# A table of ones 64 or 256 bytes wide: where the buffers behind it begin, in decay attention with two feed-forward layers

## The chip, the cores and the metric

The kernel runs on one core of one Trainium2 chip. The metric is the time of one execution on the device, in microseconds (us); lower is better. TensorE is called PE here, VectorE DVE, ScalarE ACT, GpSimd POOL and SyncE SP, as in the profile.

## The reference, cut to what matters

```python
# q, k, v: (2, 8, 768, 64) float32; lam: 8 decays; 768 tokens in blocks of 64
for b in range(nb):
    qb, kb, vb = (q[:, :, sl], k[:, :, sl], v[:, :, sl])
    intra = np.einsum('bhij,bhjd->bhid', np.einsum('bhic,bhjc->bhij', qb, kb) * Dmask[None], vb)
    inter = np.einsum('bhid,bhde->bhie', qb * lam_pow[None], kv_state)
    out[:, :, sl] = intra + inter
    kv_state = lam_block * kv_state + np.einsum('bhsd,bhse->bhde', kb * rev_pow[None], vb)
# x: the 1536 tokens by 512 channels of out
xn = x / np.sqrt(np.mean(x * x, -1, keepdims=True) + 1e-06) * rms_g
g = xn @ w_gate
x = (g * sigmoid(g) * (xn @ w_val)) @ w_out          # 512 -> 1536 -> 512
out = np.maximum(np.maximum(x @ w1, x @ w2), x @ w3) @ w_out2   # 512 -> 768 -> 512
```

All weights of the two feed-forward layers come as 64-bit floats, rms_g and the input of the attention as 32-bit ones.

## The kernel before, in words

The 1536 tokens are cut into 12 chunks of 128. For each chunk the attention is worked out in steps: `turn` transposes keys and queries on PE, `scores` multiplies them, `masked` and `next_state` run on DVE, `mixed` makes the output of the chunk, `summed` and `normed` scale it, and `rest` leaves it as a pair of a high and a low part (`xh`, `xl`), since every product of the feed-forward layers is made of three matmuls on such pairs. The first seven chunks go through a fixed interleaving ahead of the feed-forward work (the last loop of the program); the other five are slipped in between the matmuls of the first feed-forward stage (`first_stage`), which takes the first four column groups of w_gate and w_val. `second_stage` does the rest, on PE without a break.

Weights come as raw 64-bit words and are turned into a pair of 32-bit tiles in a unit of work of its own: ACT takes both halves of the words (L252, L253), DVE puts them together (L209 to L216), POOL adds (L219), ACT and POOL split the sum into a high and a low part (L180, L183). Every engine works its instructions off in the order written.

All loads are issued by SP, in one order. A chunk has three loads of 256 KB, one each for k, q and v (`load`, L92); each brings 8 runs of 256 bytes to each of 128 partitions, one run for each head. A raw weight tile of 4096 bytes a partition is brought by `load_to` (L170): for w_gate and w_val in three DMAs of runs of 1024 bytes, for the others in one DMA with runs of 1024 or 4096 bytes. The issues stand in this order at the start: k and q of chunk 0, then v, k and q of the next ones up to q of chunk 3, the first raw tile of w_gate, v of chunk 3 and so on. SP takes a load only when the buffer it goes to is free.

On-chip memory is given out by pools, one behind the other, in bytes of each partition. Pools `act` and `wp` come first; in `wp` lie three of the five buffers of raw weights. Then come `attc` (constants of the attention), `ld` (three buffers each for k and q, four for v, and two further buffers of raw weights) and `att` (working tiles of the attention). The last three are given back after the attention, and two new pools take their place from the same first byte. In `attc` each tile begins at a multiple of 32 bytes behind the last, in this order: lam8, lamh, g_sb, ones, ident, zeros, mhalf, Tm, lami, diag.

The table `ones` is set by one memset (L962) at the start, and read in one place alone, its first column as the moving operand of the matmul in `summed` (L403):

```python
nc.tensor.matmul(out=pm[:, 0:1], lhsT=d["ss"][:, a, :], rhs=ones[:, 0:1], start=a == 0, stop=a == n - 1)
```

`load_to` chooses the buffer of a raw tile by its number in the list of weights; `more` holds for numbers 3, 4, 8 and 9 alone:

```python
more = pos["load"] % 5 > 2 and pos["load"] < 3 * PLAIN - 2
t = (ld if more else wp).tile([P, KD, 2 * P], I32, tag="raw", name="wraw", bufs=2 if more else 3)
```

Of the kernel before, what the change touches and what calls it, by code (L numbers as in the profile page):

```python
# [9 lines left out]
F32 = mybir.dt.float32  # L10
# [8 lines left out]
P = 128  # L19
# [7 lines left out]
def tile_decay_attention_swiglu_maxout(  # L27
# [25 lines left out]
    C = P // 2  # L53
# [11 lines left out]
    attc = att_ctx.enter_context(tc.tile_pool(name="attc", bufs=1))  # L65
# [9 lines left out]
    lam8 = attc.tile([P, H], F32, name="lam8")  # L75
    lamh = attc.tile([P, NP], F32, name="lamh")
    g_sb = attc.tile([P, KD], F32, name="g_sb")
    ones = attc.tile([P, C // 4], F32, name="ones")
    ident = attc.tile([P, P], F32, name="ident")
    zeros = attc.tile([P, P], F32, name="zeros")  # L80
    mhalf = attc.tile([P, 1], F32, name="mhalf")
# [964 lines left out]
```

## Time and profile before

| | |
|---|---|
| median of 3 runs | 555.02 us (554.21 to 555.48) |
| the profiled execution | 553.67 us, of it 551.9 us from the first to the last instruction |
| PE busy | 534.0 us, 97% of the span |
| DVE, ACT, POOL busy | 371.4, 279.3 and 300.9 us |
| moved by DMA | 44.67 MB in 65598 packets |

The page has a strip of 40 slices of the span for each engine, for the clock that PE was granted (PEclk, in tenths of full speed) and for the DMA engines. PE is full in nearly every slice; the slices that are not full lie in the first 100 us, where chunks of the attention are worked on, and in the last. The DMA engines are busiest in the first fifth of the span and have long gaps after it.

### The profile page before, as it was taken

How to read it: one execution, taken by the hardware profiler on the slowest of the kernel's cores; microseconds unless marked ns; L12 is line 12 of the kernel's file. 1: busy time of each engine (PE TensorE's matmuls, PEld its weight loads, DVE VectorE, ACT ScalarE, POOL GpSimd, SP SyncE). 2: the span in 40 equal slices, each digit the busy share in tenths (PEclk: the TensorE clock that was granted, in tenths of full speed). 3: DMA queues.
4: the chain of work that ended last, by engine and by line, in shares of the span. 5: the costliest groups of instructions: out<-in, count | busy, mean ns of one | idle time of the engine just before them, and what ended most of it. 6: DMA issues, size and time to landing. Idle time of an engine off the chain costs nothing.

```text
span 551.9 us, 9738 instructions
## 1 busy us (share of the span) xinstructions
PE 534.0 (97%) x3728; PEld 440.6 (80%) x3728; DVE 371.4 (67%) x680; ACT 279.3 (51%) x541; POOL 300.9 (55%) x247
## 2 busy tenths in 40 slices
PE   7799997999999999999999999999999999999997
PEld 7687765878888888888888888888888888888886
DVE  4577775454886687677777685787677577684364
ACT  3576675245355556546347525646466755551120
POOL 2266886323434567475546726886386544962050
PEclk8898999999999999999999999999999999999999
DMA  9895926300111222231221312120222322210015
GB/s 183 209 225 168 220 75 133 60 3 0 39 38 40 76 76 77 77 113 41 77 76 39 114 40 76 40 76 8 69 77 83 110 76 70 84 38 1 0 40 190
DMA packets 65598, 44.67 MB, mean 81 GB/s; under 512 B 40080, under 2 KB 61840, under 8 KB 65552
## 3 DMA queue, kind: packets, MB, share of 16 engines
q1 hardware_dynamic: 64848, 44.05, 29.8%
q8 instruction: 29, 0.48, 0.4%
q14 instruction: 17, 0.14, 0.1%
q10 hardware_dynamic: 704, 0.01, 0.1%
HBM read 40.90 MB, written 3.15 MB: 80 GB/s over the span
## 4 chain that ended last, share of the span: by engine, by line
PE 84%; issue 4%; POOL 4%; DVE 2%; DMA 2%; ACT 1%; SPq 1%; POOLq 0%; ACTq 0%; DVEq 0%
PE p L683 34%; PE acc L874 9%; PE r L683 8%; PE acc L480 6%; PE acc L481 6%; PE acc L482 6%; PE pv L490 5%; PE q L683 4%; PE pg L490 4%; POOL W L219 2%; PE px L377 1%; SPq L170 1%; DMA qn<-in_q_dram 1%; POOL kd L287 1%; DMA wraw<-in_moe_w_gate_dram 1%
## 5 line engine op out<-in xcount | busy, mean ns | idle before, releaser
L183 POOL TENSOR_TENSOR wl<-W,wh 128x512 fp32r<-128x512 f32 x77 | 100.7, 1309 | 58.7 <-ACT wh L180 58.7
L219 POOL TENSOR_TENSOR W<-W,wraw 128x512 int32<-128x512 int32 x60 | 80.6, 1343 | 70.2 <-DVE W L216 66.0
L180 ACT CAST wh<-W 128x512 fp32r<-128x512 f32 x77 | 47.8, 621 | 82.3 <-POOL W L219 80.6
L501 POOL TENSOR_TENSOR hl<-sg,hh 128x512 fp32r<-128x512 f32 x36 | 47.2, 1310 | 36.1 <-ACT hh L500 36.1
L683 PE MATMUL p<-xh,wh 128*128 128x512 f32 x148 | 57.6, 389 | 0.0
L683 PE MATMUL p<-xl,wh 128*128 128x512 f32 x148 | 57.6, 389 | 0.0
L683 PE MATMUL p<-xh,wl 128*128 128x512 f32 x148 | 57.6, 389 | 0.0
L480 PE MATMUL acc<-hh,wh 128*128 128x512 f32 x144 | 56.7, 394 | 0.7 <-DVE W L216 0.7
L481 PE MATMUL acc<-hl,wh 128*128 128x512 f32 x144 | 56.2, 390 | 0.0
L482 PE MATMUL acc<-hh,wl 128*128 128x512 f32 x144 | 56.1, 390 | 0.0
L252 ACT ACTIVATE W<-wraw 128x512 f32<-128x512 f32 x60 | 40.3, 672 | 9.2 <-DMA wraw<-in_moe_w_gate_dram 5.1
L838 DVE TENSOR_TENSOR acc_sb<-acc,acc_sb 128x512 f32<-128x512 f32 x46 | 31.7, 690 | 19.5 <-PE acc L482 18.3
L209 DVE TENSOR_SCALAR mid<-W 128x512 f32<-128x512 f32 x58 | 39.7, 685 | 3.3 <-ACT W L252 3.3
L212 DVE TENSOR_SCALAR mid<-mid 128x512 int32<-128x512 int32 x58 | 40.2, 693 | 0.8
L216 DVE SCALAR_TENSOR_TENSOR W<-wraw,mid 128x512 int32<-128x512 int32 x58 | 39.5, 681 | 1.1
L253 ACT ACTIVATE wraw<-wraw 128x512 int32<-128x512 uint32 x60 | 39.8, 664 | 0.0
L738 ACT COPY c<-p 128x512 f32<-128x512 f32 x34 | 20.0, 587 | 38.3 <-PE p L683 38.3
L501 POOL TENSOR_TENSOR hl<-m,hh 128x512 fp32r<-128x512 f32 x18 | 24.1, 1345 | 23.0 <-ACT hh L500 22.9
L683 PE MATMUL p<-yh,wh 128*128 128x512 f32 x90 | 35.0, 389 | 0.0
L683 PE MATMUL p<-yl,wh 128*128 128x512 f32 x90 | 35.0, 389 | 0.0
L683 PE MATMUL p<-yh,wl 128*128 128x512 f32 x90 | 35.0, 389 | 0.0
L500 ACT CAST hh<-sg 128x512 fp32r<-128x512 f32 x36 | 22.3, 620 | 24.1 <-DVE sg L624 18.1
(176 smaller groups left out, 1327.7 us busy)
## 6 DMA issues: line engine op xcount, KB each, us to landing
wraw<-in_moe_w_out_dram SPq DMA_DIRECT2D x18, 512.0 KB, 3.4
wraw<-in_moe_w_dram SPq DMA_DIRECT2D x18, 512.0 KB, 3.5
kn<-in_k_dram SPq DMA_DIRECT2D x12, 256.0 KB, 5.3
qn<-in_q_dram SPq DMA_DIRECT2D x12, 256.0 KB, 5.5
vn<-in_v_dram SPq DMA_DIRECT2D x12, 256.0 KB, 5.3
wraw<-in_moe_w_gate_dram SPq DMA_DIRECT2D x12, 256.0 KB, 3.0
wraw<-in_moe_w_gate_dram SPq DMA_DIRECT2D x24, 128.0 KB, 3.1
wraw<-in_moe_w_val_dram SPq DMA_DIRECT2D x12, 256.0 KB, 3.1
```

The source lines that it names most:

```text
L180: nc.scalar.copy(out=wh, in_=W.bitcast(F32))
L183: nc.gpsimd.tensor_tensor(out=wl, in0=W.bitcast(F32), in1=wh.bitcast(F32), op=ALU.subtract)
L212: nc.vector.tensor_scalar(out=mid[key], in0=mid[key], scalar1=0x07FFFFFF, scalar2=3, op0=ALU.bitwise_and, op1=ALU.logical_shift_left)
L219: nc.gpsimd.tensor_tensor(out=W, in0=W, in1=lo, op=ALU.add)
L252: nc.scalar.activation(out=W.bitcast(F32), in_=hi.bitcast(F32), func=AF.Abs)
L480: nc.tensor.matmul(out=out, lhsT=wh, rhs=xh_, start=first, stop=False)
L481: nc.tensor.matmul(out=out, lhsT=wh, rhs=xl_, start=False, stop=False)
L482: nc.tensor.matmul(out=out, lhsT=wl, rhs=xh_, start=False, stop=last)
L490: nc.tensor.matmul(out=ps, lhsT=w[:, kk * P:(kk + 1) * P], rhs=x[:, kk, :], start=n == 0, stop=n == len(todo) - 1)
L501: nc.gpsimd.tensor_tensor(out=dst_l, in0=src, in1=dst_h.bitcast(F32), op=ALU.subtract)
L683: nc.tensor.matmul(out=ps, lhsT=w[:, ks], rhs=r[:, o + k, :], start=first and k == 0 and n == 0, stop=k == 1 and n == 2, skip_group_check= ...
L874: nc.tensor.matmul(out=acc[:, cs], lhsT=x[:, ts], rhs=w[:, cs], start=n == 0, stop=n == len(todo) - 1)
```

## The change

One constant gets another width. C is 64, so that `ones` has 64 columns (256 bytes a partition) where it had 16 (64 bytes).

```diff
-    ones = attc.tile([P, C // 4], F32, name="ones")
+    ones = attc.tile([P, C], F32, name="ones")
```

No instruction is added, taken away or moved on any engine; the memset of L962 writes 128x64 elements in place of 128x16. What changes is where the tiles behind `ones` begin: 192 bytes later, up to the end of the pool `att`. Taken modulo 256, the places in the two built programs are these:

| tiles | first byte mod 256 before | after |
|---|---|---|
| ident, zeros, mhalf | 32 | 224 |
| Tm, lami, diag | 64 | 0 |
| k, q, v (10 buffers of 2048 bytes) | 64 | 0 |
| raw weights in `ld` (2 buffers of 4096 bytes) | 64 | 0 |
| kT, qT, qs, kd, A, S, sq, x | 64 | 0 |
| raw weights in `wp` (3 buffers), and all else in `act` and `wp` | 128 | 128 |
| the pools that follow the attention | 128 | 128 |

A run of k, q or v is 256 bytes long, so that each one lay across a multiple of 256 before and lies between two of them after. Of 60 raw weight tiles, four (numbers 3, 4, 8 and 9 of the list) go to buffers that move.

## Rows read from the trace of the kernel before

**Rows 1.** The page: busy time by engine, and strips of 40 slices.

```profile
PE 534.0 (97%) x3728; PEld 440.6 (80%) x3728; DVE 371.4 (67%) x680; ACT 279.3 (51%) x541; POOL 300.9 (55%) x247
...
PEclk8898999999999999999999999999999999999999
DMA  9895926300111222231221312120222322210015
```

**Rows 2.** Stretches in us: busy time by engine, granted PE clock, DMA share, GB/s.

```profile
20.00:25.00 5.00, 2.84 (x18) 2.60 (x18) 2.66 (x8) 3.97 (x11) 0.00 (x0) 0.75 0.82 213
...
60.00:90.00 30.00, 26.52 (x354) 20.36 (x354) 24.68 (x58) 20.31 (x44) 23.80 (x22) 1.00 0.47 120
90.00:100.00 10.00, 7.57 (x41) 5.68 (x42) 2.66 (x8) 2.91 (x5) 6.55 (x7) 0.83 1.20 223
...
150.00:540.00 390.00, 390.00 (x1723) 322.92 (x1722) 271.90 (x436) 199.29 (x361) 223.09 (x172) 1.00 0.20 63
```

**Rows 3.** Who waited for whom, PE and ACT: us in total, times, longest.

```profile
PE pm L403 <- ACT x L390: 2.2, 1, 2.2
PE pk L297 <- DMA kn<-in_k_dram: 1.9, 1, 1.9
...
PE sc L321 <- ACT x L390: 1.5, 1, 1.5
...
PE pq L299 <- DMA qn<-in_q_dram: 0.6, 1, 0.6
...
ACT W L252 <- DMA wraw<-in_moe_w_gate_dram: 5.1, 1, 5.1
```

**Rows 4.** Timeline: start, us, engine, line, operation; idle before in brackets.

```profile
0.81 0.07 DVE L962 MEMSET ones<- 128x16 f32 x1 [0.81 <-PEq L1030]
0.86 0.17 DVE L963 MEMSET zeros<- 128x128 f32 x1
...
1.08 4.21 PE L968 MATMUL warm<-zeros 128*128 128x128 f32 x18 [1.08 <-DVE zeros L963]
...
5.94 0.42 PEld L299 LDWEIGHTS pq<-ident,qn 128*128 128x128 f32 x4 [0.32 <-DMA qn<-in_q_dram]
```

**Rows 5.** Timeline of SP's queue: the last loads ahead of the first raw tile.

```profile
10.38 1.24 SPq L92 DMA_DIRECT2D kn<-in_k_dram  x1
11.71 2.41 SPq L92 DMA_DIRECT2D qn<-in_q_dram  x1
14.17 2.37 SPq L170 DMA_DIRECT2D wraw<-in_moe_w_gate_dram  x3
```

**Rows 6.** DMA queues from 3.7 to 4.7 us: packets, MB, share of 16 engines.

```profile
q1 hardware_dynamic: 909, 0.23, 101.5%
q10 hardware_dynamic: 271, 0.00, 15.0%
```

**Rows 7.** DMA queue of SP from 73.8 to 74.3 us, a raw tile in `wp`.

```profile
q1 hardware_dynamic: 165, 0.16, 95.5%
```

**Rows 8.** DMA queue of SP from 54.8 to 55.3 us, raw tile 8, in `ld`.

```profile
q1 hardware_dynamic: 165, 0.16, 99.5%
```

**Rows 9.** DMA packets from 91.3 to 91.9 us, k of chunk 10 alone.

```profile
DMA packets 673, 0.17 MB, mean 285 GB/s; under 512 B 673, under 2 KB 673, under 8 KB 673
...
q1 hardware_dynamic: 673, 0.17, 125.6%
```

**Rows 10.** DMA packets from 5 to 14 us, k, q and v load after load.

```profile
DMA packets 7912, 1.97 MB, mean 219 GB/s; under 512 B 7911, under 2 KB 7911, under 8 KB 7911
...
q1 hardware_dynamic: 7751, 1.96, 133.5%
```

**Rows 11.** Copies of ACT by line: durations in ns, min/median/max.

```profile
L303 ACT COPY qT<-pq x12: 585/587/643, 6.6 to 110.5; 128x512 f32<-128x512 f32 x12
...
L738 ACT COPY c<-p x34: 576/587/612, 176.1 to 522.9; 128x512 f32<-128x512 f32 x34
```

**Rows 12.** Stretches round the two idle times of PE, columns as in rows 2.

```profile
23.90:27.30 3.40, 3.29 (x72) 3.09 (x75) 1.97 (x7) 2.51 (x5) 1.14 (x2) 0.50 1.01 237
27.30:30.70 3.40, 3.40 (x87) 3.28 (x82) 2.17 (x8) 1.82 (x7) 2.96 (x3) 0.70 1.14 249
...
94.30:97.70 3.40, 3.40 (x11) 2.87 (x12) 0.69 (x1) 1.16 (x3) 3.40 (x3) 0.52 1.37 222
```

## The prediction

> **What bounds the kernel now.** I read the page first, then the busy time by stretches, then the waits, then the DMA packets. The page shows PE busy for 97% of the span [rows 1]; the stretches show where the rest is: from 150 to 540 us PE is busy for the whole 390 us at full clock, with DMA at a fifth of its time [rows 2]. Nothing that the change does to a load can be felt there. PE loses time in the first 100 us, where the strip of the DMA engines is nearly full too [rows 1]. The list of waits names two places where a load of the kinds that move is the cause. Near 21 us ACT stands 5.1 us before the first raw tile of w_gate (L252); the scaling of a chunk (x, L390) is queued behind it on ACT, and PE stands 2.2 us for that [rows 3]. Near 92 us PE stands 1.9 us for k of chunk 10 and 0.6 us for its q [rows 3]. [...]
>
> **The memset.** The two memsets of DVE give a price: 0.07 us for 16 columns, 0.17 us for 128 [rows 4], so 0.10 / 112 us a column, and 48 more columns take 0.04 us. The memset of zeros and with it the 9 warming matmuls start 0.04 us later [rows 4]. The transposes follow these on PE, and the second set of them waits 0.32 us for the first q anyway [rows 4], which covers the 0.04 us; without that cover the price would be 0.04 us, under 0.01% of the time. I count nothing.
>
> **Tiles of the engines.** Does an engine work faster on a tile at a multiple of 256? ACT's copy of 128x512 takes 587 ns into qT, which lies at 64 modulo 256, and 587 ns into c, at 128 [rows 11]. Place makes no difference there, and I count nothing for kT, qs, kd, A, S, x and the constants either. Room is no matter: the pools behind the attention keep their place.
>
> **The loads: one packet.** This is the one term that can be of size. A packet is one run, and the share of the 16 engines' time gives its duration. From 3.7 to 4.7 us, 909 packets of 256 bytes took 1.015 x 16 x 1000 ns, 17.9 ns each; beside them 271 packets of 4 bytes (g_sb, on ACT's queue) took 0.150 x 16000 / 271 = 8.9 ns each [rows 6]. In a raw tile of `wp` 159 packets of 1024 bytes and 6 of 4 bytes took 0.955 x 16 x 500 ns, so 47.7 ns each [rows 7]. I count the bytes in steps of 32. From 4 to 256 bytes are 7 steps in 9.0 ns, 1.29 ns a step; from 256 to 1024 bytes are 24 steps in 29.8 ns, 1.24 ns a step. A 4-byte packet cannot lie across a multiple of 256 bytes, each run of k, q and v did. If lying across cost something, the first difference would stand out by it. At 1.24 ns a step the first 7 steps make 8.7 ns, and 0.3 ns is left for lying across. [...] The raw tiles say the same: a tile in `ld` at 64 modulo 256 takes (0.995 x 8000 - 4 x 9) / 161 = 49.2 ns a packet and one in `wp` at 128 takes 47.7 [rows 7, 8]. So the place within 256 bytes does not show; I take 0.3 ns as the saving, the row nearest to the case, with 0 and 1.0 as its near ends.
>
> [...]
>
> **The loads: a stretch.** A shorter packet helps only if packets set the pace. From 91.3 to 91.9 us, 673 packets passed 16 engines in 600 ns: one in 14.3 ns on each, less than the 17.9 ns that each takes, so they overlap [rows 9]. From 5 to 14 us 7751 packets passed in 9 us, one in 18.6 ns [rows 10]. The runs lie at the same place modulo 256 in both, so what slows the long row to 18.6 ns is not the place alone, and may well be something that the change leaves as it is. The difference, 4.3 ns, is the most that I grant the change for a packet in that row; the least is nothing.
>
> **What it comes to.** SP issues the loads of 5 to 14 us without a pause, each taking about 1.2 us or longer, and the first raw tile follows at 14.17 us [rows 5]. Ahead of it lie 7751 / 16 = 484 packets on each engine [rows 10]. At 0.3 ns they save 0.15 us of ACT's wait and so of PE's. At 92 us two loads of 64 packets on each engine save 2 x 64 x 0.3 ns = 0.04 us. The sum is 0.2 us, with 0 and 0.6 us (1.0 ns) as its ends. The profiled execution took 553.67 us, 551.9 of them its span, and would take 553.5 us; it lies 1.35 us under the median, which the change is compared with. So I take the 0.2 us from the median: 555.02 - 0.2 = 554.8 us. The runs before spread over 1.27 us, and a measurement of this kernel can tell about 0.2% (1.1 us) from no change. The forecast is no change that can be told, 553.9 to 556.1 us.
>
> **Rival 1: the packets do get shorter, and the time with them.** Mechanism: a run that lies across a multiple of 256 bytes makes two writes, and where load follows load the writes set the pace. Halfway between nothing and 4.3 ns, 2.2 ns a packet, saves 484 x 2.2 ns = 1.1 us of the 2.2 us that PE stands near 21 us, and 128 x 2.2 ns = 0.3 us near 92 us: 555.02 - 1.4 = 553.6 us. At 4.3 ns it is 2.1 + 0.55 us, and the clock may stay up. PE is busy for 6.7 us from 23.9 to 30.7 us at 0.50 and 0.70 [rows 12], (0.50 + 0.30) x 3.4 = 2.7 us of lost clock, of which I let half come back, since ACT and DVE have their own work there: 555.02 - 2.65 - 1.35 = 551.0 us. So 551.0 to 553.8 us. For it speaks that the DMA strip is full where the loads matter [rows 1]; against it the packets of 4, 256 and 1024 bytes, and that the dense row at 14.3 ns had the same place.
>
> [...]
>
> **Rival 2: slower, by one more stretch at the lower clock.** Near 84 us PE stands 1.5 us for x of ACT [rows 3], and the clock stays at 1.00 over 60 to 90 us [rows 2]; after the waits of 2.2 and 2.5 us it fell. ACT takes raw weights and x in a fixed order, so that a raw tile which lands later against the rest by 0.7 us or more would lengthen the 1.5 us to some 2.2 us, and I take that as the point from which the clock falls here too. Price: 0.7 us of idle time, and 3.4 us at half clock as in 94.3 to 97.7 us [rows 12], which loses 1.7 us: 555.02 + 2.4 = 557.4 us; if loads nearby only shift the half-clock stretch without more idle time, 556.7 us. For it speaks that every load moves a little against the compute; against it that the change makes no load longer by any row, and moves them by tenths at most.
>
> **Rival 3: it does not do what it says.** Of 60 raw tiles four move, and none of the 36 loads of k, q and v is left out; the one raw tile that ACT stands 5.1 us for is number 0, in `wp`, which keeps its place. It only comes earlier through the loads ahead of it. If place did matter for 1024 bytes alone, four tiles are all, none of them waited for in rows 3: 555.0 us. This lies within the forecast and has no share of its own.
>
> **How the numbers follow.** Forecast (0 to 0.6 us saved, and the scatter of three runs): 0.56. Rival 1: 0.29. Rival 2: 0.15. The predicted time is 554.8 us. The range reaches down to 552.4 us, which takes in rival 1 at its middle and leaves out its far end (about 0.10), and up to 556.4 us, which leaves out most of rival 2 (about 0.10). Rival 1 lies below 553.9 us nearly whole: faster 0.29; slower 0.15; same 0.56.
>
> **What would show it.** In the trace after, the share of the 16 engines and the count of packets of 3.7 to 4.7 us, of 5 to 14 us and of 91 to 92 us, worked out as here: 17.9, 18.6 and 14.3 ns again if I am right; 15 to 16 ns a packet, or a long row at 14 to 17 ns, if rival 1 is. The wait of ACT for the first raw tile should stay near 5.1 us, or fall by 1 us and more; PE's waits of 2.2, 1.9 and 0.6 us with it. The clock from 20 to 31 us and from 94 to 98 us shows what came back, and a further dip near 85 us would show rival 2. The prediction is wrong if the long row turns out to be set by the writes, or if the 0.2 us shift where a clock stretch begins.

## The result, and the profile after

The changed kernel takes 548.71 us (median of 4 runs, 547.21 to 549.46) beside 554.62 us of the kernel before on the same chip (552.30 to 555.48): a ratio of 0.9897, with an interval of 0.9858 to 0.9935. So it is faster, by 3.6 to 7.9 us, some 1%. A second comparison on another chip, with 12 runs of the changed kernel and 27 of the kernel before, gave 549.1 against 552.3 us, 0.9947 (0.9929 to 0.9965). By the medians the gain is 5.9 and 3.2 us; the second rests on more runs. The forecast was 554.8 us and no change; the range ended at 552.4 us.

The page of the kernel after, to be read beside [rows 1]: the span is 547.5 us where it was 551.9. PE has 2.8 us less of busy time, so some of its matmuls ran at a higher clock (the mean granted clock of the two profiled executions is 0.984 before and 0.991 after); the rest of the 4.4 us is idle time that has gone. In the strip of the DMA engines the first ten slices add up to 47 tenths where it was 51.

```profile
span 547.5 us, 9738 instructions
...
PE 531.2 (97%) x3728; PEld 438.5 (80%) x3728; DVE 371.3 (68%) x680; ACT 279.2 (51%) x541; POOL 301.0 (55%) x247
...
PEclk8899998999999999999999999999999999999999
DMA  8987717000201231141221212121123222200015
```

The DMA packets of the kernel after from 5 to 14 us, the stretch of [rows 10]: number, bytes, share of 16 engines.

```profile
DMA packets 8688, 2.16 MB, mean 241 GB/s; under 512 B 8687, under 2 KB 8687, under 8 KB 8687
...
q1 hardware_dynamic: 8515, 2.15, 105.8%
```

In 9 us 8515 packets passed SP's queue where 7751 did before. One passed each engine every 9000 x 16 / 8515 = 16.9 ns instead of 18.6, and took 1.058 x 16 x 9000 / 8515 = 17.9 ns instead of 24.8. From 5 to 11 us, where there are loads of k, q and v alone, the pair is 16.0 and 17.8 ns; the kernel before (the second row) has 18.5 and 24.8 ns there:

```profile
q1 hardware_dynamic: 5994, 1.51, 111.3%
```

```profile
q1 hardware_dynamic: 5195, 1.31, 134.3%
```

The two places that were to show no difference show none: from 3.7 to 4.7 us a packet takes 0.942 x 16000 / 844 = 17.9 ns, as in [rows 6], and k of chunk 10, which comes some 4 us earlier in this kernel (87.1 to 87.7 us), passes at one packet in 9600 / 676 = 14.2 ns, as in [rows 9] (first and second row):

```profile
q1 hardware_dynamic: 844, 0.21, 94.2%
...
q1 hardware_dynamic: 676, 0.17, 126.3%
```

Five more loads follow that one without a pause. The fifth load of the six, q of chunk 11, does show a difference. In the kernel before (95.5 to 96.6 us, the first row) one packet passes in 17600 / 967 = 18.2 ns and takes 25.2 ns; in the kernel after (91.3 to 91.9 us, the second row) it is 9600 / 660 = 14.5 ns and 17.9 ns:

```profile
q1 hardware_dynamic: 967, 0.24, 138.5%
```

```profile
q1 hardware_dynamic: 660, 0.17, 123.2%
```

SP issues the first raw tile at 12.54 us instead of 14.17 [rows 5], and ACT takes it up at 19.25 us. Timeline of ACT after, start, duration and, in brackets, the idle time ahead with what ended it:

```profile
19.25 0.68 ACT L252 ACTIVATE W<-wraw 128x512 f32<-128x512 f32 x1 [3.31 <-DMA wraw<-in_moe_w_gate_dram]
...
25.23 0.68 ACT L252 ACTIVATE W<-wraw 128x512 f32<-128x512 f32 x1 [1.67 <-DMA wraw<-in_moe_w_val_dram]
```

Before, the first of these stood at 21.03 us after a wait of 5.07 us:

```profile
21.03 0.67 ACT L252 ACTIVATE W<-wraw 128x512 f32<-128x512 f32 x1 [5.07 <-DMA wraw<-in_moe_w_gate_dram]
```

It is 1.78 us earlier, and PE's wait for x is 0.9 us where it was 2.2 [rows 3]. Of the waits of PE after, none names a DMA any more; near 90 us ACT has taken the place of k and q of chunk 10 (the third and fourth row, in place of 1.9 and 0.6 us):

```profile
PE sc L321 <- ACT x L390: 1.4, 1, 1.4
...
PE pm L403 <- ACT x L390: 0.9, 1, 0.9
...
PE pk L297 <- ACT wh L180: 1.3, 1, 1.3
...
PE pq L299 <- ACT kT L301: 0.8, 1, 0.8
```

Where the 4.4 us arise is seen when the same matmul is looked up in both traces. The matmul behind PE's wait for x is 1.7 us earlier in the kernel after (21.6 against 23.35 us), one at 29.2 us of before 2.8 us, one at 46.2 us 4.1 us, one at 93.1 us 4.6 us, one at 100 us 4.3 us, and the last 4.4 us. So next to nothing is gained after 50 us. The lead does not only grow: it is back to 2.2 us at 35.5 us, where PE of the kernel after waits 0.5 us for x, and 3.1 us at 43.6 us. The steps from 1.7 to 2.8 and from 3.1 to 4.1 us lie in two stretches of clock. Before, PE ran at 0.50 of its clock from 22.5 to 29.3 us, and again from 43.0 to 46.4 us; after, only from 22.5 to 25.9 us. (In both kernels a further stretch follows the idle time near 90 us.) Windows of the kernel after: us, busy time of PE, PEld, DVE, ACT and POOL, granted clock, DMA share, GB/s. The first pair answers to [rows 12]:

```profile
23.90:27.30 3.40, 3.40 (x104) 3.33 (x105) 3.24 (x12) 2.07 (x6) 2.73 (x3) 0.71 0.95 231
27.30:30.70 3.40, 3.29 (x124) 2.96 (x125) 2.62 (x8) 2.87 (x7) 1.40 (x2) 1.00 0.85 216
43.00:46.40 3.40, 3.13 (x73) 2.38 (x73) 3.40 (x7) 2.44 (x9) 1.51 (x2) 1.00 0.85 282
...
90.80:94.20 3.40, 3.40 (x9) 2.61 (x8) 0.69 (x1) 0.92 (x2) 2.44 (x2) 0.50 1.01 238
```

The third window (43.0 to 46.4 us) in the kernel before:

```profile
43.00:46.40 3.40, 3.29 (x58) 2.36 (x62) 3.05 (x8) 2.03 (x4) 3.19 (x4) 0.50 0.96 267
```

The time of one run goes with its mean granted clock. The 93 runs of the kernel before that stand beside the experiments have a median of 554.0 us where the mean clock is 0.983 to 0.985 (16 runs), 552.9 at 0.986 to 0.988 (21), 552.1 at 0.989 to 0.991 (40) and 550.8 at 0.992 to 0.994 (7): some 0.35 us for 0.001. The kernel after takes 549.5 us at 0.991 (median of 5 runs, 549.2 to 551.1) and 548.6 us at 0.993 to 0.994 (7 runs). So some 2.2 to 2.6 us of the gain are there at equal clock; the rest goes with a higher clock of the changed kernel (a mean of 0.992 over the 12 runs of the second comparison, 0.988 over the 93). This need not be a cause apart from the loads: one stretch of 3.4 us at half clock, as from 43.0 to 46.4 us, takes 0.5 x 3.4 / 552 = 0.003 off the mean of a run, and the traces have three to five such stretches in the four kernels with all loads at 64, 128 or 192 and no filling matmuls, and one to three with all loads at 0 (the last microseconds, after PE's work, left out).

### The profile page after: what moved, and what is told of

It is laid out like the page before. It is cut to its first block, busy times and chain, and to the rows that moved or that the text cites. A ratio compares the mean times of both kernels' runs of the same rounds, so it can differ in the third digit from the quotient of the medians.

```text
span 547.5 us, 9738 instructions
## 1 busy us (share of the span) xinstructions
PE 531.2 (97%) x3728; PEld 438.5 (80%) x3728; DVE 371.3 (68%) x680; ACT 279.2 (51%) x541; POOL 301.0 (55%) x247
## 4 chain that ended last, share of the span: by engine, by line
PE 86%; POOL 3%; issue 2%; DVE 2%; ACT 2%; DMA 2%; SPq 2%; POOLq 0%; ACTq 0%; DVEq 0%
PE p L683 34%; PE acc L874 9%; PE r L683 8%; PE acc L480 6%; PE acc L481 6%; PE acc L482 6%; PE pv L490 5%; PE pg L490 4%; PE q L683 4%; PE px L377 1%; SPq L92 1%; POOL W L219 1%; DMA wraw<-in_moe_w_gate_dram 1%; SPq L170 1%; PE pq L299 1%
## 5 line engine op out<-in xcount | busy, mean ns | idle before, releaser
L252 ACT ACTIVATE W<-wraw 128x512 f32<-128x512 f32 x60 | 40.3, 672 | 8.3 <-DMA wraw<-in_moe_w_gate_dram 3.8
L500 ACT CAST hh<-sg 128x512 fp32r<-128x512 f32 x36 | 22.3, 620 | 24.6 <-DVE sg L624 18.6
```

The costliest lines, as they stand in the source:

```text
L252: nc.scalar.activation(out=W.bitcast(F32), in_=hi.bitcast(F32), func=AF.Abs)
```

## Experiments

Three theories stood against each other. **A**: a run of a load that does not begin at a multiple of 256 bytes costs more on its way into the on-chip memory. **B**: the engines work faster on the tiles of `att` and `attc` that moved. **C**: PE's clock alone, for which a load that lands a little earlier is enough. Each run stands beside the kernel before on its own chip; "pace" is the time between two packets on one DMA engine from 5 to 11 us and "duration" what a packet takes there, both worked out as above.

### The loads alone, the tiles alone

`ones` keeps its 64 bytes. Empty tiles move the pool `ld` alone to 0 modulo 256 (the first), or the tiles of `att` alone (the second).

```diff
-    diag = attc.tile([P, C], F32, name="diag")
+    diag = attc.tile([P, C], F32, name="diag"); attc.tile([P, 48], F32, name="pad1"); att.tile([P, 16], F32, name="pad2", bufs=1)
```

> Only the pool of loads moves: k, q, v and two raw tiles begin at 0 modulo 256, ones stays 64 bytes wide, the constants and the working tiles of the attention stay at 64 modulo 256 (unused filler tiles of 192 and 64 bytes see to that). Theory A (runs of k, q, v that no longer lie across a multiple of 256 bytes pass faster where load follows load): the whole gain, ratio 0.990, and 16 ns or less between packets from 5 to 14 us, 18.0 ns a packet. Theory B (engines read or write the working tiles and constants faster at 0): ratio 1.000, 18.6 ns between packets and 24.8 ns a packet as before.

```diff
-    diag = attc.tile([P, C], F32, name="diag")
+    diag = attc.tile([P, C], F32, name="diag"); att.tile([P, 48], F32, name="pad2", bufs=1)
```

> Only the working tiles of the attention (kT, qT, qs, kd, A, S, sq, x) move to 0 modulo 256; k, q, v, raw tiles and constants stay at 64. Theory A: ratio 1.000 and 18.6 ns between packets from 5 to 14 us. Theory B: a ratio below 0.995 at unchanged packets.

With the loads alone: 547.48 against 552.37 us, 0.9918 (0.9897 to 0.9940); pace 15.6 ns, duration 17.8 ns. With the tiles alone: 551.72 us, 0.9992 (0.9974 to 1.0011); pace 18.4 ns, duration 24.3 ns. SP's queue from 5 to 11 us, the loads alone:

```profile
q1 hardware_dynamic: 6153, 1.55, 114.3%
```

and the tiles alone:

```profile
q1 hardware_dynamic: 5227, 1.32, 132.4%
```

The whole gain is in the loads: the first kernel leaves the constants and the tiles of `att` at their old places. Theory B falls. The loads alone were run once more beside later experiments:

> The kernel in which only the pool of loads moves to 0, once more, on the same chip as the three before: 0.990 to 0.995. It should be no slower than the changed kernel if constants and working tiles take no part.

549.82 us, 0.9936 (0.9906 to 0.9966), pace 16.7 ns. The two results agree within their intervals.

### Other places: 128, 192, and everything at 0

`ones` of 128 bytes puts the loads at 128 modulo 256, one of 192 bytes at 192. The third kernel puts a pool of 128 bytes ahead of all others, so that the raw tiles in `wp` and the later pools come to 0 too.

```diff
-    ones = attc.tile([P, C // 4], F32, name="ones")
+    ones = attc.tile([P, C // 2], F32, name="ones")
```

> ones is 32 columns wide, so that all that moves lies at 128 modulo 256: every run of k, q and v still lies across a multiple of 256, half of it on each side. Theory A in its plain form (what counts is whether a run lies across): ratio 1.000, 18.6 ns between packets from 5 to 14 us. Theory A in the form that the bytes from the multiple below are paid for (4 steps of 32 bytes in place of 2): slower, 2.4 ns more between packets, some 1.5 us or more and a ratio of 1.003 to 1.01. Theory B, if a multiple of 128 is enough for it: 0.990.

```diff
-    ones = attc.tile([P, C // 4], F32, name="ones")
+    ones = attc.tile([P, 3 * C // 4], F32, name="ones")
```

> ones is 48 columns wide, all that moves lies at 192 modulo 256: a run has 64 bytes before and 192 behind the multiple, the mirror image of the kernel before. Plain theory A: ratio 1.000, 18.6 ns between packets. Paying for the bytes below: 4.8 ns more between packets than before, ratio above 1.005. Theory B: 1.000.

```diff
+    first = ctx.enter_context(tc.tile_pool(name="first", bufs=1)); first.tile([P, 32], F32, name="pad0")
     act = ctx.enter_context(tc.tile_pool(name="act", bufs=2))
...
-    ones = attc.tile([P, C // 4], F32, name="ones")
+    ones = attc.tile([P, C // 2], F32, name="ones")
```

> An unused filler of 128 bytes ahead of all pools and ones 32 columns wide: k, q, v as in the changed kernel, and now also the three raw-weight buffers of wp, all feed-forward tiles and the output tiles at 0 modulo 256. If runs of 1024 and 4096 bytes gain from their place as runs of 256 bytes do, the mean packet of a raw tile falls from 47.7 ns and the time lies below the changed kernel's by 0.5 us or more (ratio below 0.988); if only the runs of 256 bytes in a long row gain, the time is that of the changed kernel, 0.990 to 0.992.

At 128: 552.59 us, 1.0011 (0.9994 to 1.0028), pace 18.5 ns and duration 24.5 ns. At 192: 552.74 us, 0.9998 (0.9973 to 1.0022), 18.7 and 24.3 ns. So 64, 128 and 192 are alike (18.5, 18.5 and 18.7 ns), and only 0 differs (16.0 ns): for a run of 256 bytes it is lying across a multiple of 256 that costs, whatever part of it lies on either side. The form of theory A in which the bytes from the multiple below are paid for falls: it expected 2.4 ns more than before at 128 and 4.8 at 192, and no more than 0.2 came.

All at 0: 548.21 against 552.3 us, 0.9929 (0.9908 to 0.9950); the kernel after, run beside it once more, 0.9947 (0.9929 to 0.9965). The expectation for raw tiles that gain was below 0.988; the intervals overlap, and what the raw tiles add, if anything, isn't settled.

> The changed kernel once more, on the same chip as the three before, as their measure: 0.990 within 0.985 to 0.994, 18.0 ns a packet from 5 to 14 us.

### The clock by itself

Theory C says that the clock is enough. Matmuls whose results nobody reads fill PE's idle time, and the loads stay at 64. In a first form nine of them stood ahead of L403 (chunk 1) and ten round the transposes of chunk 10:

```diff
-        pm = bank("pm")
+        pm = bank("pm"); [nc.tensor.matmul(out=pm[:, P:2 * P], lhsT=ident, rhs=ident, start=True, stop=True) for _ in range(9 if c == 1 else 0)]
```

> The kernel before (all at 64), with matmuls that only fill time on PE, 9 ahead of the sum of chunk 1 and 8 and 2 ahead of the two sets of transposes of chunk 10, where PE stands 2.2, 1.9 and 0.6 us; their results are overwritten or not read. Loads are as slow as before. If the lower clock after these two places is a real part of the gain, the half-clock stretches near 22 to 29 and 94 to 98 us go and 1 to 2.5 us come back (ratio 0.995 to 0.998). If the lower clock costs nothing because ACT and DVE set the pace there, 1.000; if filling delays the real work, above 1.000.

554.83 against 552.3 us, 1.0037 (1.0015 to 1.0059). The bank `pm` was still to be read by the very ACT work that PE waited for, so the nine ran behind the wait, from 23.07 to 27.3 us, at half clock. It was slower and told nothing of the clock. In the second form they stand ahead of the transposes of chunk 3 and of chunk 10, in a bank that is free:

```diff
-        pkv = pk.rearrange("p (a t) -> p a t", t=P)
+        pkv = pk.rearrange("p (a t) -> p a t", t=P); [nc.tensor.matmul(out=pk[:, 0:P], lhsT=ident, rhs=ident, start=True, stop=True) for _ in range({3: 9, 10: 8}.get(c, 0))]
...
+        [nc.tensor.matmul(out=pq[:, 0:P], lhsT=ident, rhs=ident, start=True, stop=True) for _ in range(2 if c == 10 else 0)]
```

> The kernel before (all at 64) with filling matmuls again, whose results are overwritten: 9 ahead of the transposes of chunk 3, which stand directly before the wait near 21 us and go to a free bank (in the first trial they were queued behind the wait), 8 and 2 ahead of the transposes of chunk 10. If the lower clock after the two places is a part of the gain that stands by itself, 1 to 2.5 us come back without any change of the loads: ratio 0.995 to 0.998, and no half-clock stretch begins near 22 us. If not, 1.000 or above.

553.14 against 552.8 us, 1.0007 (0.9989 to 1.0024). This time the clock did stay up where it used to fall, and nothing came of it. The windows of this kernel, columns as above: the clock is 1.00 from 22.5 to 25.9 us; then PE is busy for only 1.9 of 4.2 us, and the half clock comes behind that.

```profile
22.50:25.90 3.40, 3.29 (x114) 3.04 (x116) 1.02 (x4) 2.56 (x8) 0.00 (x0) 1.00 0.97 237
25.90:30.10 4.20, 1.89 (x51) 1.32 (x43) 4.20 (x14) 2.45 (x8) 4.01 (x4) 0.99 0.96 205
30.10:36.90 6.80, 6.70 (x142) 6.38 (x143) 3.42 (x10) 5.39 (x14) 4.08 (x5) 0.50 1.01 233
94.20:97.60 3.40, 1.89 (x10) 1.63 (x11) 0.52 (x1) 1.19 (x3) 3.40 (x3) 1.00 0.85 166
```

PE's waits of this kernel from 15 to 40 us, and ACT's (L251 is L252 of the kernel before):

```profile
PE pq L299 <- ACT x L390: 2.1, 1, 2.1
```

```profile
ACT W L251 <- DMA wraw<-in_moe_w_gate_dram: 5.6, 2, 5.0
ACT W L251 <- DMA wraw<-in_moe_w_val_dram: 2.6, 1, 2.6
```

Work done sooner only reaches the wait for the next raw tile sooner: ACT stands 5.0 us for the first and 2.6 us for the second, and PE stands behind it. As long as the loads land late, a higher clock there gives nothing back. The runs say the same: the median of the runs' mean granted clocks is 0.988 in the kernel before and 0.993 with the fills of the second form, and the time is the same (1.0007). Theory C falls as a cause by itself. Fills in the kernel after (4, 6 and 3 matmuls at the places of the first form, then 5, 6 and 3 at those of the second) were tried as well:

> The changed kernel with 4, 6 and 3 such matmuls at the same places. If clock and loads are separate gains they add up: 0.986 to 0.988, below the changed kernel by 1 to 2 us. If the changed kernel has already all that the clock gives, 0.990.

> The changed kernel with 5, 6 and 3 filling matmuls at these places. If clock and loads add up, 1 to 1.5 us below the changed kernel (ratio near 0.99 where the changed kernel has 0.9947 on the same chip as now); if not, the ratio of the changed kernel or above.

549.52 us, 0.9945 (0.9921 to 0.9969), and 548.63 us, 0.9921 (0.9903 to 0.9940): not to be told from the kernel after without them.

### One load in three

If each load had its own price, a kernel with v at 64 should keep two thirds of the gain, and one with v alone at 0 one third. An empty tile ahead of v in `ld` does both: 64 bytes in the kernel after, or 192 bytes in the kernel before. The two raw tiles in `ld` and the working tiles, which lie behind v, move with it.

```diff
+        (c, n) == (0, 2) and ld.tile([P, 16], F32, name="pad", bufs=1)
         t = ld.tile([P, H, D], F32, tag="kqv"[n], name="kqv"[n] + "n", bufs=4 if n == 2 else 3)
```

> The changed kernel, but with a filler of 64 bytes ahead of the buffers of v: k and q at 0 modulo 256, v, the two raw tiles behind them and the working tiles at 64. Theory A, tested load by load: from 5 to 14 us each load of k and q passes in about 1.0 us and each load of v in about 1.2; the gain is about two thirds of the whole (ratio 0.993 to 0.997). If instead something else of the changed layout sped the row up, all three are alike.

```diff
+        (c, n) == (0, 2) and ld.tile([P, 48], F32, name="pad", bufs=1)
         t = ld.tile([P, H, D], F32, tag="kqv"[n], name="kqv"[n] + "n", bufs=4 if n == 2 else 3)
```

> The kernel before with a filler of 192 bytes ahead of the buffers of v: k and q stay at 64 modulo 256, v, the two raw tiles behind and the working tiles lie at 0. Theory A with a store of writes (a slow load runs up a debt that the DMA engines hold, a fast one pays it back; the mean over loads counts): writes of k, q, v pass in (18.6 + 18.6 + 14.3) / 3 = 17.2 ns a packet, more than the 15.7 at which loads come in the changed kernel, so some debt stays: about 1.10 us a load from 5 to 11 us, packets of 18 to 22 ns, a ratio of 0.995 to 0.999. Theory C (place counts for k and q alone): 18.6 ns between packets, 1.000. Theory D (v or the raw tiles are what counts, or fewer than all misplaced loads never matter): 15.7 ns, 0.993.

With v at 64: 548.84 against 552.8 us, 0.9930 (0.9909 to 0.9952), pace 16.5 ns. With v alone at 0: 549.94 against 552.49 us, 0.9948 (0.9925 to 0.9971), pace 16.4 ns, duration 18.4 ns. SP's queue from 5 to 11 us with v at 64:

```profile
q1 hardware_dynamic: 5827, 1.47, 108.2%
```

and with v alone at 0:

```profile
q1 hardware_dynamic: 5837, 1.47, 111.8%
```

One misplaced load in three costs nothing that can be told (and the gain does not hang on the two raw tiles, which are at 64 there). Two in three cost little: ACT takes up the first raw tile at 19.92 us, where it was 21.03 before and 19.25 and 20.05 in two traces of the kernel after. The expected pace of 17.2 ns, worked out with 14.3 ns for a well placed run, did not come. A price for each load, of which one third or two thirds would be left, is not what happens.

### The loads by themselves

The last kernel leaves the whole computation out: SP alone brings 48 loads of k, q and v, six each to tiles at 0, 64, 0, 128, 0, 192, 0 and 32 modulo 256, then four raw tiles at 0 and four at 128. The two lines that set the places:

```diff
+    rows = [place(r, H * D) for r in (0, 64, 0, 128, 0, 192, 0, 32) for _ in range(6)]
+    raws = [place(r, 1024) for r in (0, 128) for _ in range(4)]
```

> Loads alone, all computation left out (the output is a copy of some of the loaded rows): 48 loads of 256 KB of k, q and v back to back on SP's queue into buffers of their own, six each at 0, 64, 0, 128, 0, 192, 0 and 32 modulo 256, then four raw tiles of w_gate at 0 and four of w_val at 128. Theory A: a load takes about 1.0 us or less in each stretch at 0 and 1.2 us at 64, 128, 192 and 32 alike from its second load on, with 24 to 26 ns a packet there. If the bytes from the multiple below were paid for, 192 would be slowest and 32 nearly as fast as 0. If place counts only beside other work on the core, all eight stretches are alike. Raw tiles: alike at 0 and 128.

SP's queue in stretches of this run: at 0 (3 to 8 us); where the row at 64 has begun (11 to 12 us); its end (12 to 15.5 us); the end of the row at 128 (26.5 to 28.8 us); at 0 again (42.2 to 48 us); the end of the row at 32 (53 to 55 us).

```profile
q1 hardware_dynamic: 5378, 1.35, 119.9%
...
q1 hardware_dynamic: 1099, 0.28, 127.5%
...
q1 hardware_dynamic: 2999, 0.76, 127.9%
...
q1 hardware_dynamic: 2048, 0.52, 126.7%
...
q1 hardware_dynamic: 5736, 1.45, 110.9%
...
q1 hardware_dynamic: 1724, 0.44, 135.7%
```

Worked out in that order, pace and duration: 14.9 and 17.8 ns; 14.6 and 18.6; 18.7 and 23.9; 18.0 and 22.8; 16.2 and 17.9; 18.6 and 25.2. In the two stretches at 0 a packet takes 17.8 and 17.9 ns, so that none is held up; what sets their pace of 14.9 and 16.2 ns is not shown. (SP spends some 0.8 to 1.8 us on a load in this run, as in the next view, but 0.43 and 0.57 us on the first two, so that SP may be held back itself.) In a misplaced row the first one to three loads still pass like the others, as from 11 to 12 us, at 14.6 ns; then the packets grow to 23 to 25 ns and the pace falls to 18 to 18.7 ns, whether at 32, 64 or 128. (At 192 packets came so slowly, one in 17.7 ns from 37 to 39 us, that little showed: 18.4 and 19.3 ns at its end. There the likeness rests on the kernel at 192 above.) SP's timeline of this run, the first two loads, two later ones to 0, and the two sets of four raw tiles:

```profile
0.73 0.43 SPq L49 DMA_DIRECT2D b<-in_k_dram  x1
1.23 0.57 SPq L49 DMA_DIRECT2D b<-in_q_dram  x1
...
39.71 1.02 SPq L49 DMA_DIRECT2D b<-in_k_dram  x1
40.77 1.04 SPq L49 DMA_DIRECT2D b<-in_q_dram  x1
...
52.78 3.07 SPq L54 DMA_DIRECT2D b<-in_moe_w_gate_dram  x4
55.90 5.25 SPq L54 DMA_DIRECT2D b<-in_moe_w_val_dram  x4
```

The raw tiles show the same with runs of 1024 bytes: 385 GB/s at 0 (58.6 to 61.2 us), still 386 GB/s in the first of the four at 128 (61.4 to 62.6 us), and 348 GB/s later at 128 (64.1 to 66.1 us).

```profile
DMA packets 1009, 1.00 MB, mean 385 GB/s; under 512 B 31, under 2 KB 1009, under 8 KB 1009
...
DMA packets 466, 0.46 MB, mean 386 GB/s; under 512 B 14, under 2 KB 466, under 8 KB 466
...
DMA packets 699, 0.70 MB, mean 348 GB/s; under 512 B 20, under 2 KB 699, under 8 KB 699
```

With the small packets left out, that is 2600 x 16 / 978 = 42.5 ns a run at 0 against 2000 x 16 / 679 = 47.1 ns at 128: 4.6 ns more for a run of 1024 bytes, where it was 3.8 ns (18.7 against 14.9) for one of 256.

So theory A holds in another form than it was put. The order of events fits this picture: a misplaced run costs work somewhere behind the packets that the profile records. That work runs on beside them and may fall behind by a load or several (14.6 ns a packet from 11 to 12 us, in a row at 64 that has just begun); only when misplaced load follows misplaced load does it hold up the packets (18.7 ns from 12 to 15.5 us). One well placed load in three gives it time to catch up, nearly (16.4 ns with v alone at 0). The picture is inferred; that there is such work, and what it is, no row shows.

The two paces that are held up fit one price. Off a multiple of 256, a run of 256 bytes lies in 2 of the stretches between multiples and one of 1024 bytes in 5; 18.7 / 2 and 47.1 / 5 are both 9.4 ns. A well placed run of 256 bytes, which lies in one, would then take 9.4 ns, and with v alone at 0 the mean would be (18.7 + 18.7 + 9.4) / 3 = 15.6 ns, less than the 16.4 ns at which packets came, so that hardly any is held up, as was found. This is an estimate from these two paces; that the price goes by such stretches, no run shows. No run has a row at 0 that is held up by this work, so the 4 ns are the distance to a pace that something else sets, and the least that a misplaced run costs more than one at 0.

## Why the prediction was wrong

**The step that failed** is in the part on a stretch: "The runs lie at the same place modulo 256 in both, so what slows the long row to 18.6 ns is not the place alone, and may well be something that the change leaves as it is." The row at 91.3 us [rows 9] is the first load after a pause. The loads alone show that the first two loads of a misplaced row are not held up (17.8 ns a packet from 10 to 11 us at 64, from 22 to 24 us at 128 and from 48 to 50 us at 32), and that only a longer row of them is (23.9 ns from 12 to 15.5 us). The two rows differed in what had gone ahead of them, and I read a difference of history as a proof that place is harmless. The row of [rows 10] was held up by its place: a packet takes 17.9 ns in place of 24.8, and the pace of 18.6 ns became 16.9, and 16.0 where k, q and v are alone. What keeps it from 14.3 ns is not shown. The trace of before had the history in it: 17.9 ns a packet from 3.7 to 4.7 us [rows 6], then 1.188 x 17600 / 978 = 21.4 ns from 4.8 to 5.9 us and 1.386 x 64000 / 3466 = 25.6 ns from 7 to 11 us (SP's queue, kernel before):

```profile
q1 hardware_dynamic: 978, 0.25, 118.8%
...
q1 hardware_dynamic: 3466, 0.87, 138.6%
```

**The price of one packet** failed with it. 0.3 ns, from packets of 4, 256 and 1024 bytes [rows 6 to 8], came from rows whose packets were not held up: the 256-byte packets of [rows 6] take 17.9 ns in both kernels, so that their duration could not hold the price. The 0.3 ns also hung on counting the bytes in whole steps of 32, a packet of 4 bytes as one, which was an assumption: no run shows such a step, and none shows the 1.0 ns that stood as the end of the term. The two rows of raw tiles, at 64 and at 128, compared two misplaced ones, and could not show the price of being misplaced. The term was to be 0.3 ns; measured in a row it is 1.7 ns here (18.6 against 16.9, from 5 to 14 us), 2.5 ns from 5 to 11 us (18.5 against 16.0) and some 4 ns where packets come fast enough (18.7 against 14.9 ns).

**Rival 1** named the mechanism as far as the runs show it (the place a run is written to sets the pace where load follows load, 18.5 ns a packet at 64 and 15.6 with the loads alone moved to 0; that a run makes two writes is not shown). Its far end, 4.3 ns and 551.0 us, was the better forecast, 4.0 us of gain where 3.2 and 5.9 were found, and I had put it at 0.10 and outside the range. That its sum comes so near is in part luck, since its terms came out otherwise. Its terms by size: it let the first raw tile come 2.1 us earlier, and 1.78 were measured; of the 0.55 us at 92 us some 0.3 came (the lead is 4.0 us at 90 us and 4.3 us at 100 us), since ACT is late next there; of the clock it gave back half of 2.7 us, and the trace shows a step of 1.1 us there (from 1.7 to 2.8 us) and a second of 1.0 us at 43 us, a stretch that I had not looked at.

**Right** were the memset (0.11 us in place of 0.07) and the tiles (the tiles alone: 0.9992), the place where loads are felt (ACT's wait for the first raw tile and PE's behind it, and nothing after 100 us), and that "the prediction is wrong if the long row turns out to be set by the writes". Rival 2 did not come: from 82 to 90 us the clock stays at 1.00, and the stretch of half clock that follows the idle time there is as long as before (3.4 us, from 90.8 to 94.2 us where it was 94.3 to 97.7). Rival 3 was right that the first raw tile gains only by the loads ahead of it, and wrong on what that is worth.

**Open** stay the exact size of the gain (the two comparisons give 0.9897 and 0.9947, and single runs scatter with their granted clock), whether the raw tiles in `wp` at 0 add something to it, and what work it is that falls behind.

## What to carry to other kernels

Where many short runs are loaded one after the other and an engine waits for what is behind them, put their buffers at multiples of 256 bytes: from 5 to 11 us a packet passed in 18.5 ns off them and in 16.0 at them here. Empty tiles do it, and with two of them the kernel took 547.48 us against 552.37. A dense row of packets is evidence for a long row only if as much of the same went ahead of it (14.3 ns after a pause and 18.6 in the long row, at the same place); when two stretches at the same place run at different pace, look at what preceded each before ruling the place out. And a lower clock behind a wait is not worth mending while the wait that caused it is set by loads: filled with matmuls, PE only met the next late tile, and the time stayed (1.0007).

## What the runs showed of the hardware

- A run that is loaded to a place off a multiple of 256 bytes in the on-chip memory costs at least some 3 to 5 ns in a row of such runs: 256 bytes nearly alike at 32, 64 and 128 (18.6, 18.7 and 18.0 ns a packet against 14.9 at 0), 1024 bytes at 128 (47.1 against 42.5 ns). The first loads of a row don't pay it at once (14.6 ns). One such load in three, or two, are hardly held up (16.5 and 16.4 ns from 5 to 11 us).
- The two held paces fit 9.4 ns for each stretch between multiples of 256 that a run lies in (18.7 / 2 and 47.1 / 5), an estimate.
- The duration of a packet does not show this price until it holds the packets up: 17.9 ns in both kernels from 3.7 to 4.7 us, then 24.8 against 17.8 ns from 5 to 11 us.
- At 0 something other than this price sets the pace, 14.9 to 16.2 ns a packet with the loads by themselves, since no packet is held up there (17.8 and 17.9 ns); what it is stays open.
- Times of one and the same kernel go with the mean granted clock of the run, by some 0.35 us for 0.001 of it. With PE's idle time filled the median of that mean rose from 0.988 to 0.993 and the time stayed (1.0007), so the clock is not the cause by itself.
